# One more DRAIN of GpSimd, behind the output scatters of the last job but one

## The chip, the cores and the metric

The kernel runs on one core of a Trainium2 chip. A core has five engines that each work through their own list of instructions: TensorE (PE in the profile, with its weight loads as PEld), VectorE (DVE), ScalarE (ACT), GpSimd (POOL) and SyncE (SP). Each has a sequencer, which fetches instructions, waits on semaphores and hands work to the engine; what the sequencer does itself carries a q in the profile (POOLq). The metric is the time of one execution on the device in microseconds; lower is better.

## The reference

The program is a retention layer (linear attention with a decay per head) followed by a mixture of experts in which each token goes to one expert.

```python
for t in range(S):                                   # B, H, S, D = 4, 8, 768, 64
    state = gamma[None, :, None, None] * state + einsum('bhd,bhe->bhde', k[:, :, t], v[:, :, t])
    y[:, :, t] = scale * einsum('bhd,bhde->bhe', q[:, :, t], state)
x = y.transpose(0, 2, 1, 3).reshape(B * S, H * D)    # 3072 tokens of 512
logits = x @ w_gate + modality_bias[modality_id]     # 8 experts
e_idx = argmax(logits, axis=1)
probs = softmax(logits); gate_w = probs[arange(N), e_idx]
for e in range(E):
    mask = e_idx == e
    h = maximum(x[mask] @ w1[e], 0.0)                # 512 -> 1024
    out[mask] = gate_w[mask, None] * (h @ w2[e])     # 1024 -> 512
```

## The kernel before, in words

The tokens are worked in 24 chunks of 128. Retention makes a chunk's rows, routing finds the place of every row in a table in device memory (`x_dram`, sorted by expert), and GpSimd scatters the rows there with an indirect DMA, one for a chunk (L485, 24 in all). Sixteen more indirect DMAs fill the rest of the experts' last slots with zero rows (L545).

The experts' work is cut into jobs of 256 rows of one expert (`SLOT`). There are 12 jobs in the list `jobs`: ten "e" jobs, which start while retention is still running, and two "s" jobs at the end. `run_job(k)` drives a job through `both`: `first_slot` makes the eight blocks of `h` (first matrix), and `second` makes the output in two halves of 128 rows (`hh` 0 and 1). To keep float32's accuracy, every operand is split into a high and a low part (`hi`, `lo`, on ScalarE and VectorE), and three products are summed on TensorE. At the end of each half, ScalarE scales the result by the gate (`o`, L871), and GpSimd scatters the 128 rows to `out` (L872). So a job issues two output scatters, and the 12 jobs issue 24: 20 named `o_e` in the profile, 4 named `o_s`.

Tokens that don't fit the 12 jobs are done in units of 32 rows (`unit`). Two of them are woven into the last two jobs, and each issues one scatter (L942, `uof_u`). A loop behind everything (L1226) would do further units; with these inputs it makes no pass, and the engines only run through its exit, where they wait for all work and all transfers. Behind that stands the program's end (L1332): each engine runs a DRAIN and reports at a barrier that GpSimd gathers and releases; GpSimd clears a range of semaphores; a second DRAIN and barrier follow.

The order on PE, ACT, DVE and SP is that in which the code is recorded (`tc.manual_schedule`). GpSimd is not in that list, and its order is set by the scheduler, with `tc.issue_after(x)` to place an instruction behind x. `s` is a job's dictionary, with its tag, its weights and rows.

Of the kernel before, what the change touches and what calls it, by code (L numbers as in the profile page):

```python
# [53 lines left out]
def kernel(  # L54
# [12 lines left out]
    nc = tc.nc  # L67
# [10 lines left out]
    def bank(name):  # L78
        return ps.tile([P, 512], F32, tag="bank", name=name)
# [97 lines left out]
    def disjoint(ins, group):  # L177

        i = getattr(ins, "ins", ins)
        tc.declare_no_dep(i, group=group, reason="rows of different tokens")  # L180
        tc.add_to_no_dep_group(group, i)
# [670 lines left out]
    def second(s):  # L852
        tag, hT = s["tag"], s["hT"]
        for hh in range(s["nh"]):
            po = bank(f"o{hh}_{tag}")
            n = 0
            for f in range(FC):
                for a, wi in PAIRS:
                    nc.tensor.matmul(  # L859
                        po,  # L860
                        hT[f][a][:, hh * P : (hh + 1) * P],
                        s["w2"][f // 2][wi][:, (f % 2) * DM : (f % 2 + 1) * DM],
                        start=(n == 0),
                        stop=(n == 3 * FC - 1),
                    )
                    n += 1
                if f % 2 and f < FC - 1:
                    yield
            o = me.tile([P, DM], F32, tag=f"o{hh}", name=f"o{hh}_{tag}")
            xg = s["xg"][hh]  # L870
            nc.scalar.activation(o, po, AF.Copy, scale=xg[:, DM + 1 : DM + 2])  # L871
            ins = nc.gpsimd.indirect_dma_start(  # L872
                out=out[:, :],
                out_offset=bass.IndirectOffsetOnAxis(
                    ap=xg.bitcast(I32)[:, DM : DM + 1], axis=0
                ),
                in_=o[:, :],
                in_offset=None,
                bounds_check=NT - 1,
                oob_is_err=False,  # L880
            )
            disjoint(ins, "out_rows")
            yield


# [67 lines left out]
    def reg(lst, i, hi):  # L953
        return nc.values_load(lst[0:1, i : i + 1], engines=[SP], min_val=0, max_val=hi)

    def start_job(j):
        kind, g, i = j
        s = dict(tag=f"{kind}{g}{i}", nh=2)
        if kind == "e":
            lst, at, n = lists[g], 0, NEV  # L960
            s["group"] = g
        else:
            lst, at, n = lists["final"], 0, NFIN
        s["at"] = [lambda h=h: reg(lst, at + h * n + i, EMPTY) for h in range(s["nh"])]
        if j is jobs[0]:
            rows_in(s)
        else:
            s["at"] = [r() for r in s["at"]]
        s["e"] = reg(lst, at + s["nh"] * n + i, NE - 1)
        return s  # L970

    def rows_in(s):
        s["xg"] = load_rows(s["tag"], s["at"], s.get("group"))
# [7 lines left out]
    def both(s):  # L981
        yield from first_slot(s)
        yield from second(s)
# [3 lines left out]
    def run_job(k):  # L987
        cur = state_of[k]
        last = k + 1 == len(jobs)
        if k == 0:  # L990
            cuts = {0: (cur, 1, 2), 1: (cur, 1, 3)}
            cuts.update({t: (cur, 2, i) for i, t in enumerate((3, 4, 6, 7))})
        else:
            cuts = {2 * i: (cur, 2, i) for i in range(4)}
        nxt = None
        for t, _ in enumerate(both(cur)):
            if t == 2 and not last:
                nxt = state_of[k + 1] = start_job(jobs[k + 1])
                raw(nxt, 1, cur)
                for i in range(4):  # L1000
                    cuts[9 + 2 * i] = (nxt, 1, i)
            if t in cuts:
                cut(*cuts[t])
            if not last:
                if t == 8:
                    rows_in(nxt)
                    raw(nxt, 2, cur)
                if t == 12:
                    flip_x(nxt)
            yield  # L1010


    jobs = [("e", g, i) for g in EVENTS for i in range(NEV)]
# [151 lines left out]
    def everything():  # L1165
# [17 lines left out]
        for n in ret:  # L1183
            tick()
            if guess is None and "guess" in lists:
                guess = dict(e=reg(lists["guess"], 0, NE - 1))
                raw(guess, 1)
                raw(guess, 2)
            if ahead is None:
                if min(EVENTS) in lists:  # L1190
                    job = state_of[0] = start_job(jobs[0])
                    raw(job, 1, guess)
                    raw(job, 2, guess)
                    ahead = AHEAD
            else:
                ahead -= 1
                if ahead in (3, 4):
                    cut(job, 1, 4 - ahead)
                if ahead == 2:
                    flip_x(job)  # L1200
                if ahead == 0:
                    break
# [134 lines left out]
```

## Time and profile before

| what | value |
|---|---|
| median of 3 runs | 433.78 us (433.01 to 434.72) |
| profiled execution, its own time | 429.9 us |
| span of the profiled execution, first to last instruction | 428.0 us |
| busy: PE, PEld, DVE, ACT, POOL | 399.8, 349.9, 247.7, 207.3, 105.5 us |
| instructions in the profile | 12025 |
| software-generated DMA (q0, issued by GpSimd) | 5184 packets, 13.67 MB |
| hardware-generated DMA (q1, issued by SP) | 25360 packets, 77.83 MB |

The busy time counts what the engines compute; what sequencers do (waits, branches, DRAINs) is not in it, and shows only where instructions are listed by source line. The span begins with the first instruction and ends with the last, the end barrier included. The profiled execution is one run; its time is 3.9 us below the median of the three timed ones.

### The profile page before, as it was taken

How to read it: one execution, taken by the hardware profiler on the slowest of the kernel's cores; microseconds unless marked ns; L12 is line 12 of the kernel's file. 1: busy time of each engine (PE TensorE's matmuls, PEld its weight loads, DVE VectorE, ACT ScalarE, POOL GpSimd, SP SyncE). 2: the span in 40 equal slices, each digit the busy share in tenths (PEclk: the TensorE clock that was granted, in tenths of full speed). 3: DMA queues.
4: the chain of work that ended last, by engine and by line, in shares of the span. 5: the costliest groups of instructions: out<-in, count | busy, mean ns of one | idle time of the engine just before them, and what ended most of it. 6: DMA issues, size and time to landing. Idle time of an engine off the chain costs nothing.

```text
span 428.0 us, 12025 instructions
## 1 busy us (share of the span) xinstructions
PE 399.8 (93%) x4596; PEld 349.9 (82%) x4596; DVE 247.7 (58%) x590; ACT 207.3 (48%) x420; POOL 105.5 (25%) x130
## 2 busy tenths in 40 slices
PE   4998849999999999999999999999999999999990
PEld 3886739989979978988988989989898989869750
DVE  1777437855745666547846856958564646536400
ACT  1244246655545545546546536546464546544320
POOL 2425211323042133012601301310873001011010
PEclk9999959999999999999999999999999999999996
DMA  8999848878788773336931314822454989993000
GB/s 284 391 386 360 308 151 263 296 256 295 260 303 275 276 257 116 121 92 233 311 112 51 125 51 157 284 102 77 129 192 141 385 291 368 407 383 136 2 25 20
DMA packets 30891, 92.79 MB, mean 217 GB/s; under 512 B 5550, under 2 KB 5678, under 8 KB 30832
## 3 DMA queue, kind: packets, MB, share of 16 engines
q1 hardware_dynamic: 25360, 77.83, 52.3%
q0 software_dynamic: 5184, 13.67, 8.6%
q8 instruction: 37, 0.61, 0.6%
q10 hardware_dynamic: 288, 0.50, 0.4%
q14 instruction: 22, 0.18, 0.1%
HBM read 94.84 MB, written 17.21 MB: 262 GB/s over the span
## 4 chain that ended last, share of the span: by engine, by line
PE 48%; issue 20%; DMA 5%; POOL 4%; DVE 3%; ACT 3%; SPq 0%; POOLq 0%; ACTq 0%
PE o_e L859 17%; PE h_e L844 17%; PE x L379 4%; PE st L267 3%; PE sc L267 3%; POOL x_dram L545 2%; ACT hi_e L784 2%; PE y L267 2%; DVE lo_e L786 2%; DMA x_dram<-zer,pad_i 2%; POOL out_dram L872 2%; PE xp_e L829 1%; DMA kv<-in_qkv_dram 1%; DMA out_dram<-o_e,xg_e 1%; DMA wa_u<-in_w_dram 1%
## 5 line engine op out<-in xcount | busy, mean ns | idle before, releaser
L786 DVE TENSOR_TENSOR lo_e<-raw,hi_e 128x1024 fp32r<-128x1024 f32 x80 | 99.7, 1247 | 86.0 <-ACT hi_e L784 85.7
L844 PE MATMUL h_e<-xTh,hi_e 128*128 128x256 f32 x320 | 91.8, 287 | 0.0
L844 PE MATMUL h_e<-xTh,lo_e 128*128 128x256 f32 x320 | 90.3, 282 | 0.0
L844 PE MATMUL h_e<-xTl,hi_e 128*128 128x256 f32 x320 | 90.3, 282 | 0.0
L784 ACT CAST hi_e<-raw 128x1024 fp32r<-128x1024 f32 x80 | 83.6, 1047 | 7.0 <-DMA raw<-in_w_dram 7.0
L859 PE MATMUL o_e<-hi_e,hTh 128*128 128x512 f32 x160 | 66.3, 414 | 0.0
L859 PE MATMUL o_e<-lo_e,hTh 128*128 128x512 f32 x160 | 63.2, 395 | 0.0
L859 PE MATMUL o_e<-hi_e,hTl 128*128 128x512 f32 x160 | 63.1, 394 | 0.0
L844 PEld LDWEIGHTS h_e<-xTh,hi_e 128*128 128x128 f32 x320 | 60.8, 190 | 0.7
L844 PEld LDWEIGHTS h_e<-xTh,lo_e 128*128 128x128 f32 x320 | 60.7, 190 | 0.3
L844 PEld LDWEIGHTS h_e<-xTl,hi_e 128*128 128x128 f32 x320 | 60.8, 190 | 0.0
L1028 POOL TENSOR_TENSOR vd<-kv,cst 128x512 f32<-128x512 f32 x24 | 27.5, 1145 | 92.7 <-DMA kv<-in_qkv_dram 36.9
L872 POOL DMA_INDIRECT out_dram<-o_e,xg_e x20 | 22.8, 1139 | 105.0 <-ACT o_e L871 84.2
L793 ACT ACTIVATE hTh<-h_e 128x256 fp32r<-128x256 f32 x80 | 30.9, 388 | 30.1 <-PE h_e L844 27.4
L401 ACT ACTIVATE xs<-x,cst 128x64 f32<-128x64 f32 x96 | 22.3, 315 | 43.6 <-DVE lh L387 25.1
L794 DVE SCALAR_TENSOR_TENSOR hTl<-h_e,hTh 128x256 fp32r<-128x256 f32 x80 | 33.0, 418 | 13.3 <-ACT hTh L793 13.2
L485 POOL DMA_INDIRECT x_dram<-xs,pos x24 | 26.9, 1119 | 46.9 <-DVE a L212 17.2
L859 PEld LDWEIGHTS o_e<-lo_e,hTh 128*128 128x128 f32 x160 | 30.1, 188 | 7.1
L859 PEld LDWEIGHTS o_e<-hi_e,hTh 128*128 128x128 f32 x160 | 30.1, 188 | 6.1
L871 ACT ACTIVATE o_e<-o_e,xg_e 128x512 f32<-128x512 f32 x20 | 13.8, 690 | 43.4 <-issue 27.9
L859 PEld LDWEIGHTS o_e<-hi_e,hTl 128*128 128x128 f32 x160 | 30.2, 189 | 5.5
L786 DVE TENSOR_TENSOR lo_s<-raw,hi_s 128x1024 fp32r<-128x1024 f32 x16 | 19.6, 1222 | 21.0 <-ACT hi_s L784 21.0
(193 smaller groups left out, 681.6 us busy)
## 6 DMA issues: line engine op xcount, KB each, us to landing
raw<-in_w_dram SPq DMA_DIRECT2D x104, 512.0 KB
kv<-in_qkv_dram SPq DMA_DIRECT2D x24, 512.0 KB
kq<-in_qkv_dram SPq DMA_DIRECT2D x23, 512.0 KB
xg_e<-x_dram SPq DMA_DIRECT2D x20, 257.0 KB
wa_u<-in_w_dram SPq DMA_DIRECT2D x8, 512.0 KB
wb_u<-in_w_dram SPq DMA_DIRECT2D x16, 256.0 KB
xg_s<-x_dram SPq DMA_DIRECT2D x4, 257.0 KB
x_dram<-xs,pos POOLq DMA_INDIRECT x24, 6.7
```

The source lines that it names most:

```text
L267: nc.tensor.matmul(out_, l, r, start=start, stop=True, skip_group_check=True)
L379: nc.tensor.matmul(px[:, g], yT[:, 2 * u + g], wgt[:, 2 * u + g], start=(g == 0), stop=(g == 1), skip_group_check=True,)
L401: nc.scalar.activation(x[:, i], px[:, i // 2, rows(i % 2)], AF.Copy, scale=gain[:, c, 4 * u + i : 4 * u + i + 1],)
L485: ins = nc.gpsimd.indirect_dma_start(out=x_dram[:, :], out_offset=bass.IndirectOffsetOnAxis(ap=pos[:, i : i + 1], axis=0), in_=xs, in_offs ...
L784: nc.scalar.copy(hi, raws[m][i])
L786: nc.vector.tensor_tensor(lo, raws[m][i], hi.bitcast(F32), op=ALU.subtract)
L793: nc.scalar.activation(hi, src, AF.Relu)
L794: nc.vector.scalar_tensor_tensor(lo, src, 0.0, hi.bitcast(F32), op0=ALU.max, op1=ALU.subtract)
L844: nc.tensor.matmul(ph, s["w1"][f // 2][wi][:, o : o + P], s["xT"][kc // 2][a][:, kc % 2, :], start=(n == 0), stop=(n == 3 * KC - 1),)
L859: nc.tensor.matmul(po, hT[f][a][:, hh * P : (hh + 1) * P], s["w2"][f // 2][wi][:, (f % 2) * DM : (f % 2 + 1) * DM], start=(n == 0), stop=( ...
L872: ins = nc.gpsimd.indirect_dma_start(out=out[:, :], out_offset=bass.IndirectOffsetOnAxis(ap=xg.bitcast(I32)[:, DM : DM + 1], axis=0), in_= ...
L1028: ins = nc.gpsimd.tensor_tensor(vds[n], vv, by[:, n % NCH].unsqueeze(2).to_broadcast([P, H, D]), op=ALU.mult)
```

## The change

In `second`, when the second half's scatter of job `jobs[-2]` (the first of the two "s" jobs) has been issued, GpSimd gets one instruction more: a DRAIN, placed right behind that scatter. `start_job` notes the job in the dictionary so that `second` can tell which one it is in. The DRAIN has no operands and waits on no semaphore and raises none. In the built program it stands on GpSimd's list between the second scatter of job `s00` and the semaphore wait that belongs to the first scatter of job `s01`. On all five engines the order of the other instructions is what it was, the four added lines moving the line numbers behind them by 4 (L942 becomes L946, L1226 becomes L1230, L1332 becomes L1336; L872 stays).

```diff
@@ second
             disjoint(ins, "out_rows")
+            if hh and s["job"] == jobs[-2]:
+
+                with tc.issue_after(getattr(ins, "ins", ins)):
+                    nc.gpsimd.drain()
             yield
@@ start_job
-        s = dict(tag=f"{kind}{g}{i}", nh=2)
+        s = dict(tag=f"{kind}{g}{i}", nh=2, job=j)
```

## The prediction

> **What bounds the kernel now.** I read the page's first two parts first, to see which engine the span follows.
>
> ```profile
> PE 399.8 (93%) x4596; PEld 349.9 (82%) x4596; DVE 247.7 (58%) x590; ACT 207.3 (48%) x420; POOL 105.5 (25%) x130
> ...
> PE   4998849999999999999999999999999999999990
> ...
> DMA  8999848878788773336931314822454989993000
> ```
>
> TensorE is busy 93% of the span; its digit is 9 in every slice from the seventh to the last but one (a slice is 428.0 / 40 = 10.7 us) and 0 in the last. GpSimd is busy 25%. So only two things can shorten the time: less for TensorE to wait for, or a shorter end after TensorE's last product. The change touches GpSimd alone, near the end, so I went to the end: the chain of waits there, and GpSimd's work in order of time.
>
> ```profile
> 390.26 20.68 issue
> ...
> 414.36 3.34 issue
> 417.70 0.50 POOLq L1225
> 418.20 0.71 POOL out_dram L872
> ```
>
> ```profile
> 389.28 0.98 POOL L872 DMA_INDIRECT out_dram<-o_s,xg_s  x1 [3.55 <-ACT o_s L871]
> 411.18 0.98 POOL L872 DMA_INDIRECT out_dram<-o_s,xg_s  x1 [20.92 <-ACT o_s L871]
> 413.48 0.88 POOL L942 DMA_INDIRECT out_dram<-uof_u,xu_u  x1 [1.32 <-ACT uof_u L941]
> 417.93 0.98 POOL L872 DMA_INDIRECT out_dram<-o_s,xg_s  x1 [3.58 <-ACTq L1226]
> ```
>
> The columns of the second are start, length, engine, line, operation and, in brackets, the idle time before. GpSimd's last scatter runs from 417.93 to 418.91, and the chain stops with it. Yet the span is 428.0: 9.1 us pass in which no engine computes. The chain doesn't speak of them, because they belong to sequencers. The line of the program's end lists them (smallest, middle and largest duration in ns, then the first and last start in us):
>
> ```profile
> L1332 SPq DRAIN  x3: 7/7/7, 421.5 to 427.4; - x3
> L1332 POOLq DRAIN  x3: 40/103/5457, 421.7 to 427.7; - x3
> L1332 ACTq DRAIN  x2: 8/8/8, 421.6 to 427.4; - x2
> L1332 DVEq DRAIN  x2: 10/14/17, 421.9 to 427.5; - x2
> L1332 PEldq DRAIN  x2: 8/8/8, 422.1 to 427.5; - x2
> ```
>
> ```profile
> L1332 POOLq DRAIN  x1: 5457/5457/5457, 421.7 to 421.7; - x1
> ```
>
> Every other engine's DRAIN takes 7 to 17 ns. GpSimd's first DRAIN behind the loop starts at 421.7, takes 5457 ns and so ends at 427.2. The four others have reported by 422.1 (TensorE is the last) and wait for it. What follows from 427.2 to 428.0 is the rest of the barrier, with two more DRAINs of GpSimd of 103 and 40 ns. So 5.46 us of the span, 1.3%, are this one instruction, and nothing lies beside it.
>
> What does it wait for? Not for data:
>
> ```profile
> core 0: us, PE busy (x) PEld busy (x) DVE busy (x) ACT busy (x) POOL busy (x), PEclk, DMA share, GB/s
> 390.26:395.73 5.47, 5.47 (x48) 5.30 (x47) 4.92 (x8) 2.97 (x5) 0.00 (x1) 1.00 0.12 48
> 395.73:411.18 15.45, 15.45 (x118) 11.31 (x117) 4.48 (x7) 5.08 (x9) 0.00 (x1) 1.00 0.01 2
> 418.91:421.72 2.81, 0.00 (x0) 0.00 (x0) 0.00 (x0) 0.00 (x0) 0.00 (x1) 0.71 0.19 69
> 421.72:427.18 5.46, 0.00 (x0) 0.00 (x0) 0.00 (x0) 0.00 (x0) 0.00 (x0) 0.50 0.00 2
> ```
>
> ```profile
> DMA to landing us min/median/max: 2.7/2.8/2.9
> ```
>
> ```profile
> L1226 POOLq EVENT_SEMAPHORE  x12: 42/43/459, 420.1 to 421.5; - x12
> ...
> L1226 POOLq INC_SWDGE_SEM  x1: 1478/1478/1478, 418.4 to 418.4; - x1
> ```
>
> The last scatter, issued at 417.93, lands at most 2.9 us later, at 420.8; the loop's exit (its longest wait 459 ns, the waits running from 420.1 to 421.5) holds GpSimd until then. In the 5.46 us of the DRAIN the DMA engines' share is 0.00 and all five engines are idle. So GpSimd itself works, on something that has piled up, or that costs a fixed time. The only work of GpSimd that can leave something behind is the indirect DMA, whose transfers the profile lists on a queue that it calls software_dynamic (packets, MB, share):
>
> ```profile
> q0 software_dynamic: 5184, 13.67, 8.6%
> ```
>
> ```profile
> L485 POOL DMA_INDIRECT x_dram<-xs,pos x24 | 26.9, 1119 | 46.9 <-DVE a L212 17.2 <-DVE xs L451 12.8 <-DVE hTl L794 6.6
> L872 POOL DMA_INDIRECT out_dram<-o_e,xg_e x20 | 22.8, 1139 | 105.0 <-ACT o_e L871 84.2 <-DMA wa_u<-in_w_dram 16.0 <-DMA raw<-in_w_dram 3.6
> L545 POOL DMA_INDIRECT x_dram<-zer,pad_i x16 | 18.3, 1145 | 14.5 <-issue 14.2 <-DMA out_dram<-o_e,xg_e 0.3
> L872 POOL DMA_INDIRECT out_dram<-o_s,xg_s x4 | 3.9, 980 | 49.0 <-ACT o_s L871 45.4 <-ACTq L1226 3.6
> ...
> L942 POOL DMA_INDIRECT out_dram<-uof_u,xu_u x2 | 1.8, 882 | 3.5 <-ACT uof_u L941 3.5
> ```
>
> ```profile
> L1322 POOLq DRAIN  x1: 189/189/189, 0.3 to 0.3; - x1
> ```
>
> 24 + 20 + 16 + 4 + 2 = 66 scatters stand between the DRAIN of 189 ns at the program's start and the one of 5457 ns; none stands between that and those of 103 and 40 ns. A DRAIN with no scatter since the last is thus short, and the one with 66 is long. If the excess is per scatter, it is (5457 - 189) / 66 = 80 to (5457 - 40) / 66 = 82 ns: I take 81.
>
> **The change part by part.** It adds one DRAIN to GpSimd's list, moves no other instruction and adds no DMA and no semaphore.
>
> *The added DRAIN.* It comes after the scatter that ends at 389.28 + 0.98 = 390.26. 63 scatters are behind it by then (66 less the three at 411.18, 413.48 and 417.93). By count it costs 63 x 81 ns + 0.04 to 0.19 = 5.2 us. If it also waits for the newest scatter to land, the longest landing of the lines below adds 7.6 us after 389.28, and it ends at 402.1.
>
> ```profile
> DMA to landing us min/median/max: 2.7/3.7/7.6
> ```
>
> Queued behind it on GpSimd are only a register move, a semaphore wait and the scatter at 411.18, which stood idle 20.92 us for ScalarE's `o_s`. The cover is the chain's 20.68 us row (390.26 to 410.94). The DRAIN ends 8.8 to 15.5 us before it. No other engine waits on GpSimd in that stretch: its next output is that scatter. Cost on the path: 0. Were the cover gone, it would cost its whole 5.2 us.
>
> *The final DRAIN.* This is the term that the change lives on, and no row shows it with few scatters behind it. Its bounds: from below the 103 and 40 ns of the DRAINs with none, from above the 5457 ns unchanged. I take the count: 3 x 81 + 40 to 189 = 0.28 to 0.43, about 0.36 us, since it lies between the rows with 0 and with 66 and is nearest to those with 0.
>
> The Trainium skill has a rule that speaks against this: "PSUM — Partial Sum Buffer", section "Engine vs sequencer instructions", says that a DRAIN waits for the engine to go fully idle. By that rule alone a DRAIN at 421.7, when nothing runs, would take next to nothing, and another one before it would change nothing; the 5457 ns row disagrees with it. Another page of the Trainium skill, "VectorE: DVE Perf Modes", section "The DRAIN you can't avoid", gives some 12 ns for a DRAIN at a program's start or end on every engine; the 7 to 17 ns of the other four agree, GpSimd's don't. By these two pages of the Trainium skill the sum below would be 0: no change.
>
> *What is late next.* GpSimd would be through at 421.7 + 0.36 = 422.08, and TensorE's report comes at 422.1. So the barrier would be complete at about 422.15 in place of 427.2, and the 0.8 us of barrier that follow are as before: the span ends at 422.95.
>
> *The scatters behind it.* The last three start with no backlog. A scatter takes 0.98 us; the very long ones average 1.14. The last, at 417.93, waits for ScalarE, and the landing that the loop's exit waits for isn't GpSimd's work. I book 0, within 0.2 us either way.
>
> *Sum.* 428.0 - 422.95 = 5.05 us less. The profiled execution took 429.9, so it would take 424.85. Against the median shown, 433.78, which is 3.9 us above the profiled run, the forecast is 433.78 - 5.05 = 428.7. A term at the very end of the program is the same in either, so I subtract it in microseconds.
>
> **The rivals.**
>
> *The final DRAIN is fixed once any scatter has been issued* (it looks through all 16 DMA engines' queues, say: 5.46 / 16 = 0.34 each). Then the added one costs the same under its cover, the last one stays at 5.46, and the time is 433.8. For it: a single long DRAIN can't tell a fixed price from one by count. Against it: the DRAINs of 189, 103 and 40 ns show that GpSimd has no long fixed price without a scatter ahead, and the last scatter alone, which landed 0.9 us before the DRAIN began, leaves no row that could be 5.46 us of work. The Trainium skill, "GPSIMD Engine Reference", section "2.1 Instruction dispatch", has another fixed price: the first call of code that has just been loaded costs about 6 us, with no instruction of its own in the profile. By that rule three scatters between the two DRAINs could bring the load back, again no change; the 189 ns at the start show no such load. The idle-engine rule above ends here too, at 433.8, and has its chance in this case's.
>
> *Part fixed, part by count.* Half of the 5.46 stays: 2.7 less 0.2, so 2.5 us are saved and the time is 431.3.
>
> *Slower: the DRAIN shuts VectorE out.* From 390.26 to 395.73 VectorE is busy 4.92 of 5.47 us with the splits that feed TensorE, which is busy all of it. If the DRAIN kept VectorE from working until it ends, waiting for the landing included (402.1 at the latest), TensorE would stall by up to 402.1 - 390.3 = 11.8 us, and the sum is 11.8 - 5.05 = 6.8 more: 440.5. It decides from a hold of 5.05 + 2.2 = 7.3 us on (the 2.2 is half a per cent, below). Against it: a DRAIN has no operands, and in the long one at the end no VectorE work lies beside it that could show a hold. The Trainium skill, "SBUF — State Buffer", section "Who interferes with whom", says that GpSimd and some VectorE instructions exclude each other at a shared port; no run here shows that for a DRAIN.
>
> **How the numbers follow.** The backlog by count gets 0.66, the fixed price 0.20, the mixture 0.09, the shut-out 0.05. The time is that of the first, 428.7. Its own range is 427.4 to 430.2: 0.3 us for the scatters and the barrier, and about 1 us for the scatter of the runs (433.01 to 434.72 around 433.78). The range for 8 in 10 reaches from there through the mixture and into half of the fixed case: 427.4 to 434.0. A measurement of this kernel can tell 0.5%, 2.2 us, from no change. Faster: 0.66 and 0.05 of the mixture's 0.09, 0.71. Same: 0.20 and the mixture's other 0.04, 0.24. Slower: 0.05.
>
> **What the profile of the changed kernel would show.** The added line has a DRAIN of GpSimd that starts near 390.3 and takes 5 us or more, and the end's first DRAIN falls from 5457 to 280 to 430 ns: then the count is right. If that one still takes 5.4 us, the fixed price is right, whatever the added one takes. TensorE's digits and the start of the scatter near 411.2 should stay. I would be wrong if the added DRAIN were short (the backlog is worked off at the end only), if VectorE's or TensorE's stretch from 390 to 402 grew, or if another engine's report came later than 422.1.

## The result, and the profile after

The changed kernel is faster by the 5 us forecast. Beside runs of the kernel before it took 429.09 us (median of 6) against 434.02 (median of 5), a ratio of 0.9885 (95% interval 0.9865 to 0.9905). A sixth run of the kernel before, of 440.45 us, fell in a slower state of the chip and is left out. In a later comparison on a chip where both are quicker it took 424.07 against 429.20, 0.9884 (0.9869 to 0.9899). The difference is 4.9 and 5.1 us; the intervals reach 0.9 and 0.6 us to either side.

The end of the program, as it was shown of before: the sequencers' DRAINs (smallest, middle, largest in ns, first and last start in us), then the added DRAIN, which the profile lists under L886.

```profile
L1336 SPq DRAIN  x3: 7/7/7, 425.8 to 426.6; - x3
L1336 POOLq DRAIN  x3: 46/103/302, 426.0 to 426.9; - x3
L1336 ACTq DRAIN  x2: 8/8/8, 425.9 to 426.6; - x2
L1336 DVEq DRAIN  x2: 10/14/17, 426.1 to 426.6; - x2
L1336 PEldq DRAIN  x2: 8/8/8, 426.3 to 426.7; - x2
```

```profile
L886 POOLq DRAIN  x1: 6437/6437/6437, 393.4 to 393.4; - x1
```

The 5457 ns are gone: GpSimd's first DRAIN behind the loop takes 302 ns, and the barrier is done within a microsecond of TensorE's report at 426.3. GpSimd's scatters in order of time, what GpSimd's sequencer does in the loop's exit, and the stretches of the added DRAIN and of the last one:

```profile
393.61 0.98 POOL L872 DMA_INDIRECT out_dram<-o_s,xg_s  x1 [3.55 <-ACT o_s L871]
415.51 0.97 POOL L872 DMA_INDIRECT out_dram<-o_s,xg_s  x1 [20.92 <-ACT o_s L871]
417.80 0.88 POOL L946 DMA_INDIRECT out_dram<-uof_u,xu_u  x1 [1.32 <-ACT uof_u L945]
422.26 0.98 POOL L872 DMA_INDIRECT out_dram<-o_s,xg_s  x1 [3.58 <-ACTq L1230]
```

```profile
L1230 POOLq EVENT_SEMAPHORE  x12: 42/43/1657, 423.2 to 425.8; - x12
...
L1230 POOLq INC_SWDGE_SEM  x1: 219/219/219, 422.8 to 422.8; - x1
```

```profile
core 0: us, PE busy (x) PEld busy (x) DVE busy (x) ACT busy (x) POOL busy (x), PEclk, DMA share, GB/s
...
393.37:399.81 6.44, 6.44 (x56) 6.27 (x55) 5.00 (x8) 4.19 (x7) 0.98 (x1) 1.00 0.18 69
...
394.59:399.81 5.22, 5.22 (x46) 5.05 (x45) 4.71 (x8) 2.97 (x5) 0.00 (x0) 1.00 0.14 53
...
423.24:426.00 2.76, 0.00 (x0) 0.00 (x0) 0.00 (x0) 0.00 (x0) 0.00 (x1) 0.67 0.19 70
426.00:426.30 0.30, 0.00 (x0) 0.00 (x0) 0.00 (x0) 0.00 (x0) 0.00 (x0) 0.50 0.00 0
```

The added DRAIN is dispatched at 393.37, while its scatter is still ahead of it (393.61 to 394.59), and ends at 399.81, so 5.22 us behind the scatter's end. In those 5.22 us TensorE is busy all the time and VectorE 4.71 us, or 90%, as in the same stretch before (4.92 of 5.47). GpSimd stood idle 20.92 us before the next scatter, for ScalarE, to the hundredth as before. From the start of the last scatter to the last instruction it is 427.2 - 422.26 = 4.9 us; before, 428.0 - 417.93 = 10.1. So the end gave 5.1 us.

The two spans differ by 0.8 us only, because the profiled execution of before had been a quick one: its last scatter started 4.3 us earlier than that of after. The stages ahead of the last two jobs, which the change doesn't touch, vary that much from profile to profile: in the second profile of the changed kernel, further below, the last scatter starts 4.8 us earlier than in this one.

### The profile page after: what moved, and what is told of

Its sections match the earlier page's. It is cut to its first block, busy times and chain, and to the rows that moved or that the text cites. A ratio compares the mean times of both kernels' runs of the same rounds, so it can differ in the third digit from the quotient of the medians.

```text
span 427.2 us, 12026 instructions
## 1 busy us (share of the span) xinstructions
PE 403.8 (95%) x4596; PEld 352.8 (83%) x4596; DVE 247.5 (58%) x590; ACT 207.7 (49%) x420; POOL 103.1 (24%) x130
## 4 chain that ended last, share of the span: by engine, by line
PE 54%; issue 17%; DMA 5%; DVE 3%; POOL 3%; ACT 2%; POOLq 1%; SPq 0%; ACTq 0%
PE o_e L859 20%; PE h_e L844 20%; PE x L379 4%; PE st L267 3%; PE sc L267 3%; PE y L267 2%; DVE lo_e L786 2%; PE xp_e L829 2%; ACT hi_e L784 1%; DMA kv<-in_qkv_dram 1%; POOL out_dram L872 1%; POOL x_dram L545 1%; DMA x_dram<-zer,pad_i 1%; DMA xg_e<-x_dram 1%; DMA wa_u<-in_w_dram 1%
## 5 line engine op out<-in xcount | busy, mean ns | idle before, releaser
L872 POOL DMA_INDIRECT out_dram<-o_e,xg_e x20 | 20.6, 1032 | 110.2 <-ACT o_e L871 90.4
L379 PE MATMUL x<-wgt,yT 128*128 128x144 f32 x192 | 30.7, 304 | 1.8 <-issue 1.8
```

What stands on the lines that cost most here:

```text
L379: nc.tensor.matmul(px[:, g], yT[:, 2 * u + g], wgt[:, 2 * u + g], start=(g == 0), stop=(g == 1), skip_group_check=True,)
L872: ins = nc.gpsimd.indirect_dma_start(out=out[:, :], out_offset=bass.IndirectOffsetOnAxis(ap=xg.bitcast(I32)[:, DM : DM + 1], axis=0), in_= ...
```

## The experiments

Three theories were open once the result was known. By **count**, a DRAIN costs so many ns for each indirect DMA that GpSimd issued since its last one. By **first time**, the first DRAIN behind any scatter pays a fixed price once in a run. By **elapsed time**, it costs more the longer the last DRAIN is ago. The changed kernel's 302 ns after three scatters had already refuted a fixed price for every DRAIN with scatters ahead. All times below are against runs of the kernel before on the same chip (medians of 428.7 to 429.3 us). Edits are shown against the changed kernel, unless it is said otherwise.

**The kernel before, profiled once more** (no edit).

> The kernel before once more, for a second profile. By the count (about 81 ns for each indirect DMA that GpSimd has issued since its last DRAIN, and 40 to 100 ns besides) the end's first DRAIN takes 5.4 to 5.5 us again, however long the rest of the span is. If its length followed the transfers in flight or the time of the run, it would differ by some tenths of a us. The first profile of before was 3.9 us under its median; if that was this one execution's luck in the stages ahead of the last two jobs, this one's last job starts some 4 us later.

```profile
L1332 POOLq DRAIN  x3: 40/103/5457, 423.3 to 429.3; - x3
```

```profile
419.52 0.98 POOL L872 DMA_INDIRECT out_dram<-o_s,xg_s  x1 [3.58 <-ACTq L1226]
```

One run, 431.47 us, span 429.6. The DRAIN is 5457 ns again, to the nanosecond, while the last scatter starts 1.6 us later than in the first profile (I had expected some 4). From that start to the end it is again 429.6 - 419.52 = 10.1 us. So the length belongs to what the program did, not to the run's speed.

**The DRAIN behind the first job.**

```diff
-            if hh and s["job"] == jobs[-2]:
+            if hh and s["job"] == jobs[0]:
```

> The added DRAIN stands behind the second scatter of the first job instead of the last but one: 11 indirect DMAs lie before it, 55 behind it. Count: the added one takes 11 x 81 + 100 ns = 1.0 us from the end of its scatter, the end's first DRAIN 55 x 81 + 100 ns = 4.5 to 4.6 us, and the time falls by 0.9 us (0.2%, within the noise). Rival, a price paid once in a run at the first DRAIN behind any scatter: the added one takes 5.4 us, the last 0.1 to 0.3 us, and the time falls by 5 us. Rival, a price by the time since the last DRAIN: 4.1 us at the end.

```profile
L1336 POOLq DRAIN  x3: 52/103/4553, 421.3 to 426.4; - x3
```

```profile
L886 POOLq DRAIN  x1: 7147/7147/7147, 99.9 to 99.9; - x1
```

```profile
L872 POOL DMA_INDIRECT out_dram<-o_e,xg_e x1: 981/981/981, 100.2 to 100.2; - x1
...
DMA to landing us min/median/max: 6.4/6.4/6.4
```

The end's DRAIN takes 4553 ns with 55 scatters issued since the last DRAIN, 904 ns less than with 66: 82 ns for each of 11. First time (0.1 to 0.3 us) falls, and elapsed time had said 4.1 us. The added DRAIN itself I missed: not 1.0 us but 5.9 us from its scatter's end (99.9 + 7.15 = 107.05, less 101.14). The scatter, started at 100.16, lands 6.4 us later, at 106.6; the DRAIN ends 0.5 us behind that. So a DRAIN waits for the newest scatter to land. In time it is 428.70 against 429.28, ratio 0.9994 (0.9981 to 1.0007): the 0.9 us expected, a ratio of 0.9979, lies just outside the interval, so the time doesn't show the gain. The profile's end does: 426.7 - 417.69 = 9.0 us from the start of the last scatter, against 10.1.

**The DRAIN behind the last job.**

```diff
-            if hh and s["job"] == jobs[-2]:
+            if hh and s["job"] == jobs[-1]:
```

> The added DRAIN stands behind the very last scatter, where nothing covers it but that scatter's own landing (2.9 us from its start) and the loop's exit. All 66 lie before it. If a DRAIN works the list off at once, it takes 5.4 us from the end of the scatter, the exit's own steps (about 2 us) follow it, the end's DRAIN is 0.04 to 0.1 us, and the time falls by about 0.8 us. If it first waits for the landing, it ends 1.9 us later, 7.3 us behind the scatter's end, and the time rises by about 1 us.

```profile
L1336 POOLq DRAIN  x3: 34/43/103, 427.2 to 427.8; - x3
```

```profile
L886 POOLq DRAIN  x1: 6682/6682/6682, 418.2 to 418.2; - x1
```

```profile
418.40 0.98 POOL L872 DMA_INDIRECT out_dram<-o_s,xg_s  x1 [3.58 <-ACTq L1230]
```

```profile
DMA to landing us min/median/max: 2.8/2.8/2.8
```

The end's DRAIN, with no scatter since the added one, is 43 ns. The added one starts at 418.2 and ends at 424.9, 5.5 us behind its scatter's end (419.38). The landing at 421.2 adds nothing to 66 x 82 ns = 5.4 us, so with a long list work goes on beside the landing. The loop's exit then follows, and from the start of the last scatter to the end it is 428.0 - 418.40 = 9.6 us, 0.5 less than before where 0.8 were expected. The time shows no change: 1.0000 (0.9989 to 1.0012). So here, where no idle time of GpSimd covers it, the added DRAIN gains nothing that can be measured.

**Twenty scatters more, no DRAIN added.** Each output scatter of the "e" jobs is issued a second time, to `spare`, another table in device memory. The edit is shown against the kernel before.

```diff
             disjoint(ins, "out_rows")
+            if s["job"][0] == "e":
+                more = nc.gpsimd.indirect_dma_start(out=spare[:, :], ...)   # as the one above
+                disjoint(more, "spare_rows")
```

> No DRAIN is added. Each of the 20 output scatters of the ten e jobs is issued a second time, to a spare table of the same shape in device memory, so 86 indirect DMAs stand before the end's first DRAIN. Count: it takes 86 x 81 + 100 ns = 7.0 to 7.1 us, and the time rises by 1.6 us (0.4%), if the 5 MB more of writes and GpSimd's 20 us more of work are hidden beside TensorE. By time, or fixed: 5.46 us as before and no change.

```profile
L1345 POOLq DRAIN  x3: 40/103/7091, 426.6 to 434.2; - x3
```

```profile
325.23 0.98 POOL L546 DMA_INDIRECT x_dram<-zer,pad_i  x1 [0.30 <-issue]
```

```profile
322.66 0.98 POOL L545 DMA_INDIRECT x_dram<-zer,pad_i  x1 [0.30 <-issue]
```

7091 ns, 1634 more for 20 scatters, 82 ns each, over nearly the same stretch of time: elapsed time falls again, and count stands. The time rose by more than the 1.6 us: 436.49, ratio 1.0156 (1.0125 to 1.0188), by the ratio 6.7 us. The other 5 us come from the middle. The last two rows shown are the last of the sixteen scatters of zero rows, here (L546) and in the second profile of before (L545). It starts 2.6 us later here. With ScalarE's 420 instructions of the two profiles matched one to one, this run is 1.7 us ahead of that one up to 322 and 3.0 us behind from 338 on: 4.7 us are lost in that stretch, where the added scatters stand between those of the zero rows on GpSimd's list. SyncE, which loads the jobs' rows (`xg_e`) from `x_dram`, waits 14.5 us for the zero rows here and 8.8 us in the second profile of before. My assumption that they were hidden was wrong there.

**The change again, on a chip where both kernels are quicker.**

> The changed kernel once more, on a chip on which the kernel before takes about 429 us. If the gain lies in the end alone, it is the same 5.0 us in absolute terms whatever the stages ahead take: ratio 0.988. From the start of the last scatter to the last instruction the profile shows 4.9 us, against 10.1 before. Rival, that the first comparison's 5 us came from the stages ahead of the last jobs (which differ by some us from profile to profile): a ratio near 1.00.

```profile
L1336 POOLq DRAIN  x3: 46/103/302, 421.0 to 421.9; - x3
```

```profile
417.49 0.98 POOL L872 DMA_INDIRECT out_dram<-o_s,xg_s  x1 [3.58 <-ACTq L1230]
```

0.9884 (0.9869 to 0.9899), and 422.2 - 417.49 = 4.7 us from the last scatter's start to the end. The gain of the first comparison was not luck in the stages ahead.

**Twenty scatters more, and the change.** The edit is shown against the twenty more.

```diff
+            if hh and s["job"] == jobs[-2]:
+                with tc.issue_after(getattr(ins, "ins", ins)):
+                    nc.gpsimd.drain()
```

> The kernel with 20 scatters more to a spare table, and the added DRAIN of the change: 83 indirect DMAs lie before it, 3 behind. Count: the added one takes 83 x 82 + 60 ns = 6.9 us from the end of its scatter (20.7 us are free), the end's first DRAIN 0.3 us, and the time is 6.8 us below that of the 20 more alone (436.5), so 429.7, since the change takes a larger sum out of the end. A fixed gain would give 431.4.

```profile
L1349 POOLq DRAIN  x3: 46/103/302, 427.0 to 428.0; - x3
```

```profile
L899 POOLq DRAIN  x1: 8070/8070/8070, 393.9 to 393.9; - x1
```

302 ns again, and the added DRAIN takes 8070 ns, of which some 1.2 us go to its own scatter, as in the change: 6.85 us for 83 scatters. The time is 430.10 (ratio 1.0019, 1.0005 to 1.0033), 6.4 us below that of the twenty more alone where count said 6.8 and a fixed gain 5.1. The two ran in different comparisons, each beside before (429.20 and 429.28), and the runs of the twenty more reach from 433.35 to 438.00, so the times can't tell 6.8 from 5.1. What decides for count is the end's DRAIN: 7091 ns there, 302 here.

**A DRAIN behind every half of the first eleven jobs.**

```diff
-            if hh and s["job"] == jobs[-2]:
+            if s["job"] != jobs[-1]:
```

> A DRAIN of GpSimd behind every output scatter of the first eleven jobs (22 of them), none in the last job. If a DRAIN waits for the newest scatter to land as well as working off the list, each takes the longer of 82 ns a scatter and the landing (2.7 to 7.6 us), so 3 to 8 us, and up to 100 us of GpSimd go to them. The end's first DRAIN is 0.3 us as in the change. If GpSimd's idle time covers the waits, the ratio is 0.988; if the scatters of the table or the retention's products behind them are held up, it is worse by some us, up to no gain.

```profile
L886 POOLq DRAIN  x22: 3035/5534/10312, 94.6 to 396.7; - x22
```

```profile
L1336 POOLq DRAIN  x3: 46/103/298, 428.0 to 428.8; - x3
```

```profile
315.74 0.98 POOL L545 DMA_INDIRECT x_dram<-zer,pad_i  x1 [3.21 <-issue]
...
326.58 0.98 POOL L545 DMA_INDIRECT x_dram<-zer,pad_i  x1 [2.84 <-issue]
327.86 0.98 POOL L545 DMA_INDIRECT x_dram<-zer,pad_i  x1 [0.30 <-issue]
```

```profile
L810 SPq DMA_DIRECT2D xg_e<-x_dram x2: 333/333/333, 330.0 to 330.6; - x2
```

```profile
L810 SPq DMA_DIRECT2D xg_e<-x_dram x2: 333/333/333, 324.9 to 329.0; - x2
```

```profile
SPq L810 <- DMA x_dram<-zer,pad_i: 16.2, 1, 16.2
```

```profile
SPq L810 <- DMA x_dram<-zer,pad_i: 8.8, 1, 8.8
```

The end keeps its 0.3 us, but the ratio is 1.0040 (1.0027 to 1.0052), 6.8 us worse than the change. Two DRAINs fell between the sixteen scatters of zero rows and left GpSimd idle 3.21 and 2.84 us there, each time for a landing. The next rows to be loaded, `xg_e`, wait for those scatters: SyncE waits 16.2 us (the first of the last two rows) against 8.8 in the second profile of before, and the two loads are issued at 330.0 and 330.6, against 324.9 and 329.0. By ScalarE's instructions, matched as above, this run is 1.5 us ahead of that profile up to 322 and 4.6 us behind from 338 on. So 6.1 us are lost in that stretch, and the lag doesn't grow under the DRAINs that follow.

**The same without the two among the zero rows.**

```diff
-            if s["job"] != jobs[-1]:
+            if s["job"] not in (("e", 5, 1), jobs[-1]):
```

> The 22 DRAINs of the run before, less the two behind the scatters of job e51, which stood among the 16 scatters of zero rows and left GpSimd 3.21 and 2.84 us idle there. If the whole loss of that run (6.8 us against the change) was made there, the ratio is back at 0.988. If the other DRAINs, 3 to 9 us of GpSimd each, cost the path as well, it stays between 0.988 and 1.004.

```profile
L886 POOLq DRAIN  x20: 3037/4714/10068, 92.5 to 388.8; - x20
```

```profile
L810 SPq DMA_DIRECT2D xg_e<-x_dram x2: 332/332/333, 323.0 to 325.8; - x2
```

0.9894 (0.9876 to 0.9911), which can't be told from the change's 0.9884: next to nothing of the loss is left, with 20 DRAINs of 3 to 10 us in place of one. So it was lost at those two places, and the idle time of GpSimd covers the other 20.

**A second DRAIN in the last job,** behind the unit's scatter.

```diff
         if tag != "dyn":
             disjoint(ins, "out_rows")
+        if tag == f"u{NTAIL - 1}":
+            with tc.issue_after(getattr(ins, "ins", ins)):
+                nc.gpsimd.drain()
```

> The change, and a second DRAIN in the last job, behind the unit's scatter: one scatter is left for the end. Count: the end's first DRAIN takes 82 + 60 = 0.14 us in place of 0.30. TensorE's report comes about 0.3 us after that DRAIN's start in any case, so the end gains nothing or 0.1 us: ratio 0.988 as the change.

```profile
L1339 POOLq DRAIN  x3: 46/103/128, 421.7 to 422.6; - x3
```

```profile
L958 POOLq DRAIN  x1: 2379/2379/2379, 413.3 to 413.3; - x1
```

128 ns with one scatter left. The second row is the second added DRAIN, with two scatters on its list; it ends 0.1 us behind the landing of the unit's. The time is 424.02, 0.9878 (0.9864 to 0.9892), the change's within the measurement. No version tried beats the change by anything that can be told.

## Why the prediction was right

The chain of steps held, in order.

- *What bounds the end.* The single DRAIN of GpSimd, with all else idle, was the term, and its removal is the gain: 5.1 us of the end by the profile, 4.9 and 5.1 by the two comparisons, 5.05 forecast. That the times agree with the forecast to a tenth or two is partly luck, since their intervals reach 0.9 and 0.6 us to either side; the profile's end is the sharper sign.
- *The price.* Five lengths of the end's DRAIN now stand on one line:

| scatters since the last DRAIN | 1 | 3 | 55 | 66 | 86 |
|---|---|---|---|---|---|
| ns | 128 | 302 | 4553 | 5457 | 7091 |

  From 3 to 55 it is 81.8 ns each, from 55 to 66 82.2, from 66 to 86 81.7, and 302 - 3 x 82 leaves 56 ns. Two other runs with 3 scatters gave 298. The 81 that I took from a single row and a subtraction was right; 0.36 us was forecast and 0.30 came.
- *The cover.* The added DRAIN's 5.22 us lie in GpSimd's 20.9 us of idleness. It took the 5.2 by count, so nothing was added for its scatter's landing, which this profile doesn't list. In the second profile of the change it ended 5.35 us behind the scatter's end, 0.1 us more, which the last section explains.
- *What is late next.* TensorE's report at 426.3 against the DRAIN's end at 426.3: both in the same tenth.
- *The rivals.* A fixed price is out (3 scatters give 0.30, 55 give 4.55). The mixture is out with the 56 ns. VectorE was not shut out: it was busy 4.71 of the DRAIN's 5.22 us behind its scatter, and TensorE all of it.
- *Too loose:* whether a DRAIN waits for the landing I left open with a bound of 402.1, the landing and then the whole list. It does wait, but only half of the list is left for after the landing (last section). That matters elsewhere (the experiment among the zero rows), not here.
- *The base.* I took the gain off the median, not off the profiled time, and said why. The other chip bears that out: 4.9 us off 434.0 and 5.1 off 429.2.

The rule of the Trainium skill, "PSUM — Partial Sum Buffer", section "Engine vs sequencer instructions", that a DRAIN waits for the engine to go fully idle, doesn't by itself foretell the length here: with every engine's work done and every transfer landed, GpSimd's DRAIN at the end took 43 to 7091 ns, by the number of scatters since the last DRAIN. The 6 us of the Trainium skill's "GPSIMD Engine Reference", section "2.1 Instruction dispatch", for the first call of code that has just been loaded show in none of these DRAINs: their lengths follow from the number of scatters and the landing.

## What to carry to other kernels

List the sequencers' instructions of the program's last lines, not only the engines' work: a long DRAIN there is counted in no busy time and stands in no chain. Where GpSimd issues many indirect DMAs, issue one DRAIN in its last long idle stretch, far enough ahead of its next job to hold 82 ns for each of them, or the newest one's landing and 41 ns for each, whichever is longer. Where GpSimd itself is on the path, as among the zero rows here, a DRAIN costs about its whole wait: 3.21 and 2.84 us of waiting, some 6 us lost.

## What the runs showed of the hardware

- GpSimd's DRAIN at the end, with all transfers landed, costs 82 ns for each indirect DMA since its last one, and about 56 ns besides. Whether a scatter has 128 rows or a unit's 32 made no difference that these sums show: from 1 to 3 scatters (one of 128 rows and one of 32 more) it grows by 174 ns.
- Behind a fresh scatter, half of that work goes on beside the transfer, and the other half comes only when the newest scatter has landed. Of the added DRAINs whose scatter's landing is in the profile, those with a short list all ended that much behind it:

  | scatters since the last DRAIN | 1 | 2 | 3 | 4 | 6 | 10 | 11 | 19 |
  |---|---|---|---|---|---|---|---|---|
  | ns from the landing to the DRAIN's end | 72 to 83 | 115, 124 | 160 | 203 to 205 | 282 | 449 to 455 | 495 | 817 |

  That is 41 ns, half of 82, for each scatter, and about 35 ns besides. With 63 in the second profile of the change the landing came 2.74 us behind the scatter's end, just later than half of the list (63 x 41 ns = 2.6 us), and the DRAIN ended 2.62 us behind the landing, 5.35 us behind the scatter's end. With 66 behind the last job the landing came earlier than half of the list (1.8 us against 2.7), and it took the 5.5 us of the count. The rows of the DRAIN with 19 (in the version without the two among the zero rows) and of the one with 63, each with its scatter's time to landing; the scatters start at 327.86 and 388.84:

```profile
L886 POOLq DRAIN  x1: 8270/8270/8270, 327.6 to 327.6; - x1
```

```profile
DMA to landing us min/median/max: 7.2/7.2/7.2
```

```profile
L886 POOLq DRAIN  x1: 6570/6570/6570, 388.6 to 388.6; - x1
```

```profile
DMA to landing us min/median/max: 3.7/3.7/3.7
```

- The semaphore step that the loop's exit issues on GpSimd (INC_SWDGE_SEM) also grows with the list: 160 ns with none, 219 with 3, 1478 with 66. It cost nothing in the kernel before, since it ended at 419.9 and the exit waits for the last landing at 420.8.

```profile
L1230 POOLq INC_SWDGE_SEM  x1: 160/160/160, 425.6 to 425.6; - x1
```
